# Turning attention probabilities: two 128-lane VectorE transposes and 16 ScalarE copies in place of 16 32-lane VectorE transposes

## The chip, the core and the metric

The kernel runs on one core of one Trainium2 chip. The metric is the device time of one execution in microseconds (us); the value shown is the median of the timed runs. All operands in memory are fp32.

## The reference

Attention with keys and values averaged over groups of 8 positions, and then a feed-forward block with softplus, for batch 8, 8 heads, 576 positions, head size 64 (4608 tokens of 512 numbers, inner size 2048):

```python
k_p = k.reshape(B, H, 72, 8, D).mean(axis=3)
v_p = v.reshape(B, H, 72, 8, D).mean(axis=3)
scores = (q @ k_p.transpose(0, 1, 3, 2)) / sqrt(D)
attn = exp(scores - scores.max(-1))
attn = attn / (attn.sum(-1) + 1e-09)
x = (attn @ v_p) laid out as [B * S, H * D]
h = x @ w_in
g = maximum(h, 0) + log1p(exp(-abs(h)))
out = g @ w_out
```

## The kernel before, in words

The 4608 tokens are cut into 18 chunks of 256 (two tiles of 128 tokens, T = 2). For each chunk there is an attention part and a feed-forward part. The feed-forward part splits every fp32 operand into a high and a low part and multiplies three times. From chunk 4 on (NF) its second product goes through seven smaller products of sums (`pair2_fast`). A chunk has eight steps u of the feed-forward part; a step is 24 matmuls of the first product (`pair1`, line 771) and 21 of the second (`pair2_fast`, line 911). TensorE (PE) runs the first product of step u + 1 ahead of the second product of step u, so that the engines between the two have one step's time. That work between is, per step: on ScalarE (ACT) the softplus `g` (779), the same rounded, `gh` (793), and the rounded sums `so` (836); on VectorE (DVE) the sums `sf` (829 to 831), `gl` (800) and the low part of `so` (841).

While chunk c is in its feed-forward part, the attention of chunk c + 1 is worked through beside it. Its scores stand in a tile E of 128 tokens by 16 rows of (half of the heads, head pair, tile, parity r) by 72 pooled keys. `exponential` (328) raises them, `sum` (579) and `reciprocal` (583, 584) give one factor for each of the 16 rows, and `scale` (603) multiplies. For the product with the values (`av_products`, 690 for the first 64 pooled keys, 697 for the last 8), P must stand with the keys on the partitions, in the tile pT. From chunk 6 on (WIDE), that is done without TensorE:

- `scale(0, False)` (608) is one VectorE instruction over the 8 rows of parity 0; `scale(n, True)` (606) is one ScalarE instruction for each of the 8 rows of parity 1.
- `turn_main` (638) is 16 VectorE transposes. Each takes one quarter of the partitions (32 tokens, i) and 32 of the 64 keys of one parity (f), for all 8 blocks, and writes them to partitions 32f to 32f + 31 of pT, so it crosses from quarter i to quarter f.
- `ends_of` (614), `turn_ends` (622), `ends_high` (627), `ends_low` (631) and `last_high` (663) do the same for the last 8 keys. They are as before after the change.

On TensorE the attention of the next chunk stands between steps 6 and 7 of a chunk: first the scores of chunk c + 1 (518; two small pieces of them are copied out of PSUM by line 552 on VectorE and line 550 on ScalarE), then `av_products(c + 1)`, both in one fixed order with the feed-forward steps (`before`). Chunk 17, the last, has only the `av_products` there.

What each engine does in which order is worked out when the kernel is built, by a list planner (`Order.run`, line 53): every operation has an engine, an estimated cost, operations that it follows, and buffers ("slots") out of named kinds. The planner takes the engine on which something could end first, and on it, of what could start within a pause, the operation with the longest chain of costs behind it; `first` adds to that rank (HURRY, 60, for the feed-forward work on ScalarE and VectorE). The transposes have no such addition. Slots of kind G are six tiles of 512 fp32 per partition, used by `g`, `sf`, the output tiles, `kept` and `le`. On the chip each engine then runs its list in that order, and waits on semaphores for the other engines.

Of the kernel before, what the change touches and what calls it, by code (L numbers as in the profile page):

```python
# [9 lines left out]
F32 = mybir.dt.float32  # L10
# [3 lines left out]
ALU = mybir.AluOpType  # L14
# [16 lines left out]
class Order:  # L31
# [11 lines left out]
    def op(self, engine, cost, fn, after=(), slots=(), lag=None, rest=0, first=0, table=None):  # L43
        o = Op(engine, cost, fn, after, slots, self.HOP if lag is None else lag, len(self.ops))
        o.rest, o.first, o.table = rest, first + self.first, table
        for x in o.after:
            x.followers.append(o)
        for x in slots:
            x.users.append(o)
        self.ops.append(o)  # L50
        return o
# [54 lines left out]
def pooled_attention_softplus_ffn(  # L106
# [9 lines left out]
    nc = tc.nc  # L116
    nc.scalar.preload_act_table_set("exp_and_others")
    B, H, S, D = q.shape
    NTOK, DM = out.shape
    DFF = w_in.shape[1]  # L120
    P = 128
    POOL = 8
    SP = S // POOL
    KM = 64
    KL = SP - KM
    T = 2
    CT = T * P
    HP = H // 2
# [17 lines left out]
    one = ctx.enter_context(tc.tile_pool(name="one", bufs=1))  # L146
# [167 lines left out]
    qt_, x_, e_, pt_, last_ = {}, {}, {}, {}, {}  # L314
# [3 lines left out]
    def ones():  # L318
        x = one.tile([P, T, H, SP], F32, tag="E", name="ones").rearrange("p t h y -> p (t h y)")
        nc.vector.memset(x[:, 0:512], 1.0)  # L320
        return x
# [5 lines left out]
    def exponential(E):  # L327
        nc.scalar.activation(out=E, in_=E, func=AF.Exp, scale=-1.0)
# [175 lines left out]
    class Chunk:  # L504
# [95 lines left out]
                    in0=split(self.E()[:, :, KM:SP])[:, e],  # L600
                    in1=split(self.sm.unsqueeze(2).to_broadcast([P, T * H, KL]))[:, e], op=ALU.mult)

        def scale(self, n, by_scalar):
            r = slice(n, None, 2)
            if by_scalar:
                nc.scalar.mul(self.E()[:, n], self.E()[:, n], self.sm[:, n:n + 1])
            else:
                nc.vector.tensor_tensor(
                    out=self.E()[:, r], in0=self.E()[:, r],
                    in1=self.sm[:, r].unsqueeze(2).to_broadcast([P, T * HP, SP]), op=ALU.mult)  # L610

        def ends_of(self, tag):
            self.pe = one.tile([P, 2 * T, R], F32, tag=tag, name="pe")
# [17 lines left out]
            nc.vector.tensor_tensor(out=x[R:2 * R], in0=self.le[0:R], in1=x[0:R].bitcast(F32),  # L631
                                    op=ALU.subtract)

        def turn_main(self, i, f):
            if i == f == 0:
                pt_[self.c] = one.tile([P, HP, CT], F32, tag="Z", name="pT")
            r, w = slice(32 * i, 32 * (i + 1)), slice(f % 2 * 32, f % 2 * 32 + 32)
            nc.vector.transpose(  # L638
                out=pt_[self.c].rearrange("p n (t i) -> p (n t) i", t=T)[32 * f:32 * f + 32, :, r],
                in_=self.E().rearrange("p (b r) y -> p b r y", r=2)[r, :, f // 2, w])  # L640

        def PT(self, pss):
            for t, ps in enumerate(pss):
# [290 lines left out]
    def load_wi(c, u):  # L934

        for k in range(2):
# [10 lines left out]
    op = todo.op  # L947
    ACT, DVE, PE, SYNC, POOLQ = (nc.scalar.engine, nc.vector.engine, nc.tensor.engine, nc.sync.engine,
                                 nc.gpsimd.engine)
# [9 lines left out]
    def act(n):  # L959
        return 0.14 + 0.00094 * n  # L960
# [4 lines left out]
    def dve2(n):  # L965
        return 0.14 + 0.00106 * n
# [384 lines left out]
    o = op(DVE, 0.3, lambda: x_w.append(ones()), first=2000)  # L1351
# [117 lines left out]
    op = todo.op  # L1469
# [102 lines left out]
    def probabilities(c, where):  # L1572
        x, s_E, subs = chunks[c]
        ex = op(ACT, 1.2 + TABLE, lambda: exponential(e_[c]), [*subs, where], [s_E])
        op(ACT, TABLE, lambda: None, [ex], first=5000)
        s_lt, s_pT, s_sm, s_pe = Slot("lt_"), Slot("pT"), Slot("sm"), Slot("ld")
        s_pm = [Slot("G") for _ in range(0 if c >= WIDE else T)]
        o = op(DVE, 1.33, lambda: x.sum(s_sm.name), [ex], [s_E, s_sm])
        o = op(DVE, 0.4, x.reciprocal, [o], [s_sm])
        if c >= WIDE:  # L1580
            s_le = Slot("G")
            parts = [op(DVE, dve2(576), lambda: x.scale(0, False), [o], [s_E, s_sm])]
            parts += [op(ACT, 0.25, lambda n=n: x.scale(n, True), [o], [s_E, s_sm])
                      for n in range(1, T * H, 2)]
            e = op(ACT, 0.25, lambda: x.ends_of(s_pe.name), parts, [s_E, s_pe])
            main = [op(DVE, dve2(256), lambda i=i, f=f: x.turn_main(i, f),
                       parts[:1] if f < 2 else parts[1:], [s_E, s_pT])
                    for i in range(P // 32) for f in range(4)]
            le = [op(DVE, 0.3, lambda i=i: x.turn_ends(i, s_le.name), [e], [s_pe, s_le])
                  for i in range(P // 32)]  # L1590
            h = op(ACT, act(512), x.ends_high, le, [s_le, s_lt])
            lo = op(DVE, dve2(512), x.ends_low, [h], [s_le, s_lt])
            again = op(ACT, act(512), lambda: x.last_high(2, None), [h], [s_lt])
            late_values[c] = [*main, lo, again], s_lt, s_pT
            return
        e = [op(DVE, 0.7, lambda t=t: x.main(t, s_pm[t].name), [o], [s_E, s_sm, s_pm[t]])
             for t in range(T)]
        e.append(op(DVE, 0.3, lambda: x.ends(s_pe.name), [o], [s_E, s_sm, s_pe]))
        chosen[c] = x, e, s_pm, s_pe, s_lt, s_pT
# [168 lines left out]
    for c in range(N1, NCH + 1):  # L1768
# [5 lines left out]
        for u in range(FP):  # L1774
# [6 lines left out]
            if c < NCH:  # L1781
                if u == 1 and c + 1 <= ALONE + 1:
                    only_scores(c + 1, before if c > N1 else None)
                before = first_products(c, u, before)
                if u == (SOON if c + 1 >= max(WIDE, ALONE + 2) else EXP) and c + 1 < NCH:
                    probabilities(c + 1, third[c, u])
                    if c + 1 <= ALONE:
                        turn_p(c + 1)
                        values(c + 1)
                if u == 4 and ALONE <= c < NCH - 1:  # L1790
                    before = turn_p(c + 1, before)
# [44 lines left out]
```

## Time and profile before

| | us |
|---|---|
| three timed runs | 867.51, 872.35, 879.10 |
| median | 872.35 |
| span of the profiled execution, first to last instruction | 867.6 |
| TensorE busy in it | 846.9 (98%) |
| VectorE busy | 738.7 (85%) |
| ScalarE busy | 422.4 (49%) |
| twelve stretches in which chunks 6 to 17 get their attention (284.77 to 819.57) | 534.8 |

The profiled execution has no time of its own beside its span; the span lies 0.1 us from the lowest timed run and 4.7 us under the median. Busy time of TensorE is not work at its peak: matmuls are pipelined and their ends are modelled, so a short wait can hide inside a busy stretch and shows better as a later start of the next group.

### The profile page before, as it was taken

The numbers are of one execution on the slowest core, as the hardware profiler recorded it, in microseconds if no ns is written. First come the engines' busy times: TensorE is split into PE (matmuls) and PEld (weight loads), VectorE is DVE, ScalarE is ACT, GpSimd is POOL, SyncE is SP. The second block draws the span as 40 slices with busy tenths as digits, with TensorE's granted clock in tenths as the row PEclk, the third lists the DMA queues.
The fourth block names the chain that finished last, engine by engine and source line by source line (L and its number), as shares of the span: only waits on it lengthen the run. The fifth ranks groups of instructions, "written<-read, shape, count | busy, mean of one in ns | idle before, by whom it ended". The sixth has DMA issues, their size and how long they took to land.

```text
span 867.6 us, 20471 instructions
## 1 busy us (share of the span) xinstructions
PE 846.9 (98%) x8056; PEld 803.5 (93%) x8056; DVE 738.7 (85%) x1609; ACT 422.4 (49%) x912; POOL 157.0 (18%) x291
## 2 busy tenths in 40 slices
PE   7999999999999999999999999999999999999997
PEld 3789989889889999999999999999999999999997
DVE  5999999878896898988899999999998997878654
ACT  5954433354444635363735455445545463636332
POOL 1000000004632313021522234123512130000000
PEclk9999999999999999999999999999999999999999
DMA  8974634546788768685677767595769574647572
GB/s 241 318 243 159 206 122 140 186 173 187 245 287 268 238 227 262 227 262 207 220 262 241 257 202 272 198 278 186 272 201 279 191 241 173 232 159 243 184 248 76
DMA packets 88704, 191.14 MB, mean 220 GB/s; under 512 B 23328, under 2 KB 39712, under 8 KB 88608
## 3 DMA queue, kind: packets, MB, share of 16 engines
q1 hardware_dynamic: 79904, 183.00, 63.3%
q0 software_dynamic: 8704, 6.83, 3.1%
q8 instruction: 63, 1.03, 0.5%
q14 instruction: 33, 0.27, 0.1%
HBM read 167.25 MB, written 22.54 MB: 219 GB/s over the span
## 4 chain that ended last, share of the span: by engine, by line
PE 88%; DVE 5%; DMA 3%; ACT 2%; issue 1%; SPq 0%; DVEq 0%; ACTq 0%
PE h L771 36%; PE m L911 29%; PE acc L745 7%; PE h L723 7%; PE avp L690 2%; PE acc L812 2%; DMA w<-wi 2%; PE avp L697 1%; ACT E L440 1%; DMA t<-t 1%; PE sc L518 1%; DMA q<-in_q_dram 1%; PE kps L1150 1%; DVE pT L638 1%; DVE kst L227 0%
## 5 line engine op out<-in xcount | busy, mean ns | idle before, releaser
L771 PE MATMUL h<-x,w 128*128 128x256 f32 x2880 | 349.0, 277 | 1.5 <-DVE x L707 1.2
L771 PEld LDWEIGHTS h<-x,w 128*128 128x128 f32 x2880 | 337.8, 188 | 3.1 <-issue 1.6
L373 POOL DMA_DIRECT2D q<-in_q_dram x272 | 154.6, 572 | 558.5 <-DMA w<-t 192.2
L911 PE MATMUL m<-w,so 128*128 128x256 f32 x1344 | 174.3, 277 | 0.5 <-ACT so L836 0.2
L779 ACT ACTIVATE g<-h 128x512 f32<-128x512 f32 x120 | 71.9, 600 | 205.3 <-PE h L771 205.0
L911 PEld LDWEIGHTS m<-w,so 128*128 128x128 f32 x1344 | 162.6, 188 | 1.2 <-ACT so L836 0.4
L911 PE MATMUL m<-w,gh 128*128 128x256 f32 x672 | 126.2, 277 | 0.0
L836 ACT CAST so<-sf 128x512 fp32r<-128x512 f32 x112 | 69.5, 621 | 80.8 <-DVE sf L831 73.3
L911 PEld LDWEIGHTS m<-w,gh 128*128 128x128 f32 x672 | 101.5, 188 | 0.0
L841 DVE TENSOR_TENSOR so<-sf,so 128x512 fp32r<-128x512 f32 x112 | 77.1, 689 | 22.2 <-ACT so L836 21.3
L911 PE MATMUL m<-w,gl 128*128 128x256 f32 x336 | 93.0, 277 | 0.0
L638 DVE STREAM_TRANSPOSE pT<-E 32x256 f32<-32x256 f32 x192 | 83.7, 436 | 3.1
L829 DVE TENSOR_TENSOR sf<-g 128x256 f32<-128x256 f32 x112 | 47.5, 424 | 42.0 <-ACT g L779 38.8
L723 PEld LDWEIGHTS h<-x,w 128*128 128x128 f32 x576 | 71.8, 188 | 3.6 <-DVE w L1051 0.6
L723 PE MATMUL h<-x,w 128*128 128x256 f32 x576 | 73.2, 279 | 0.3 <-DVE w L1051 0.3
L800 DVE TENSOR_TENSOR gl<-g,gh 128x384 fp32r<-128x384 f32 (+1 forms) x120 | 67.1, 559 | 1.3 <-ACT w L877 0.8
L728 ACT ACTIVATE g<-h 128x256 fp32r<-128x256 f32 x96 | 32.2, 383 | 65.6 <-PE h L723 46.2
L911 PEld LDWEIGHTS m<-w,gl 128*128 128x128 f32 x336 | 63.2, 188 | 0.0
L745 PE MATMUL acc<-w,g 128*128 128x512 f32 x192 | 60.9, 398 | 0.0
L793 ACT ACTIVATE gh<-h 128x384 fp32r<-128x384 f32 (+1 forms) x120 | 59.1, 493 | 0.0
L932 DVE TENSOR_TENSOR o<-o,m 128x256 f32<-128x256 f32 x98 | 39.6, 417 | 3.3 <-ACT o L924 0.4
L745 PEld LDWEIGHTS acc<-w,g 128*128 128x128 f32 x192 | 33.3, 188 | 5.4
(215 smaller groups left out, 977.9 us busy)
## 6 DMA issues: line engine op xcount, KB each, us to landing
w<-wi SPq DMA_DIRECT2D x224, 512.0 KB
out_dram<-o SPq DMA_DIRECT2D x36, 256.0 KB
wst<-in_moe_w_in_dram SPq DMA_DIRECT2D x32, 256.0 KB
wst<-in_moe_w_out_dram SPq DMA_DIRECT2D x16, 512.0 KB
wi<-w SPq DMA_DIRECT2D x16, 512.0 KB
kst<-in_k_dram SPq DMA_DIRECT2D x24, 288.0 KB
vst<-in_v_dram SPq DMA_DIRECT2D x24, 256.0 KB
t<-t SPq DMA_DIRECT2D x9, 512.0 KB
```

Source lines behind the costliest of these rows:

```text
L373: nc.gpsimd.dma_start(out=q_quarters(c)[32 * f:32 * (f + 1), m, g], in_=src[2 * m + f // 2, :, :, f % 2 * 32:f % 2 * 32 + 32])
L638: nc.vector.transpose(out=pt_[self.c].rearrange("p n (t i) -> p (n t) i", t=T)[32 * f:32 * f + 32, :, r], in_=self.E().rearrange("p (b r) ...
L723: nc.tensor.matmul(out=ps[:, 0:CT], lhsT=row(w, kc), rhs=x[:, kc], start=first and kc == j == 0, stop=last and kc == KC - 1 and j == 2)
L745: nc.tensor.matmul(out=accs[c][t], lhsT=a[:, ts], rhs=w, start=f == 0 and j == 0, stop=f == FC - 1 and j == 2)
L771: nc.tensor.matmul(out=ps[:, k * CT:(k + 1) * CT], lhsT=row(w, kc), rhs=x_[c][i][:, kc], start=first and n == 0, stop=last and n == len(or ...
L779: nc.scalar.activation(out=g, in_=x.rearrange("p (b i) -> p b i", i=P), func=AF.Softplus)
L793: nc.scalar.activation(out=gh, in_=quarters(c, x.rearrange("p (b i) -> p b i", i=P)), func=AF.Softplus)
L800: nc.vector.tensor_tensor(out=gl, in0=quarters(c, g), in1=gh.bitcast(F32), op=ALU.subtract)
L829: tt(out=sf[:, 0:3:2], in0=g[:, 0:1].to_broadcast([P, 2, P]), in1=g[:, 1:3], op=ALU.subtract)
L836: nc.scalar.copy(out=so[:, 0], in_=ss[c, u])
L841: nc.vector.tensor_tensor(out=so[:, 1], in0=sf, in1=so[:, 0].bitcast(F32), op=ALU.subtract)
L911: nc.tensor.matmul(out=ms[c][n], lhsT=x, rhs=y, start=u == 0 and j == 0 and n in (1, 6, 5, 4), stop=u == FP - 1 and j == 2 and n in (2, 7, ...
```

## The change

From chunk 6 on, both parities are scaled by one VectorE instruction each. Then for each parity r one VectorE transpose over all 128 partitions (`turn_in`) turns the 32 by 32 blocks in place of quarters into a new tile pq (512 fp32 per partition, a G slot), and eight ScalarE copies (`spread`) carry each 32-partition quarter of pq, 256 numbers a partition, to the quarter of pT where it belongs. The planner is told 0.38 us for each copy.

```diff
-        def scale(self, n, by_scalar):
+        def scale(self, n):
             r = slice(n, None, 2)
-            if by_scalar:
-                nc.scalar.mul(self.E()[:, n], self.E()[:, n], self.sm[:, n:n + 1])
-            else:
-                nc.vector.tensor_tensor(
+            nc.vector.tensor_tensor(
...
-        def turn_main(self, i, f):
-            if i == f == 0:
+        def turn_in(self, r, tag):
+
+            x = self.pm[r] = one.tile([P, T * HP, 2, 32], F32, tag=tag, name="pq")
+            nc.vector.transpose(
+                out=x, in_=self.E().rearrange("p (b r) y -> p b r y", r=2)[:, :, r, 0:KM].rearrange(
+                    "p b (k w) -> p b k w", w=32))
+
+        def spread(self, r, k, i):
+            if self.c not in pt_:
                 pt_[self.c] = one.tile([P, HP, CT], F32, tag="Z", name="pT")
-            r, w = slice(32 * i, 32 * (i + 1)), slice(f % 2 * 32, f % 2 * 32 + 32)
-            nc.vector.transpose(
-                out=pt_[self.c].rearrange("p n (t i) -> p (n t) i", t=T)[32 * f:32 * f + 32, :, r],
-                in_=self.E().rearrange("p (b r) y -> p b r y", r=2)[r, :, f // 2, w])
+            f, w = 2 * r + k, slice(32 * i, 32 * (i + 1))
+            nc.scalar.copy(
+                out=pt_[self.c].rearrange("p n (t i) -> p (n t) i", t=T)[32 * f:32 * f + 32, :, w],
+                in_=self.pm[r][w, :, k])
...
-            parts = [op(DVE, dve2(576), lambda: x.scale(0, False), [o], [s_E, s_sm])]
-            parts += [op(ACT, 0.25, lambda n=n: x.scale(n, True), [o], [s_E, s_sm])
-                      for n in range(1, T * H, 2)]
+            parts = [op(DVE, dve2(576), lambda n=n: x.scale(n), [o], [s_E, s_sm]) for n in range(2)]
             e = op(ACT, 0.25, lambda: x.ends_of(s_pe.name), parts, [s_E, s_pe])
-            main = [op(DVE, dve2(256), lambda i=i, f=f: x.turn_main(i, f),
-                       parts[:1] if f < 2 else parts[1:], [s_E, s_pT])
-                    for i in range(P // 32) for f in range(4)]
+            main = []
+            for r in range(2):
+                s_r = Slot("G")
+                o = op(DVE, dve2(512), lambda r=r, s=s_r: x.turn_in(r, s.name), [parts[r]], [s_E, s_r])
+                main += [op(ACT, 0.38, lambda r=r, k=k, i=i: x.spread(r, k, i), [o], [s_r, s_pT])
+                         for k in range(2) for i in range(P // 32)]
```

## Rows read from the trace of the kernel before

**Rows 1.** The page: its first line and busy time of TensorE.
```profile
span 867.6 us, 20471 instructions
...
PE 846.9 (98%) x8056; PEld 803.5 (93%) x8056; DVE 738.7 (85%) x1609; ACT 422.4 (49%) x912; POOL 157.0 (18%) x291
```

**Rows 2.** Busy time by stretch, one per chunk: stretch, its length, busy us (instructions) of PE, PEld, DVE, ACT, POOL; PEclk.
```profile
461.17:505.23 44.06, 44.06 (x450) 43.26 (x450) 40.60 (x95) 21.80 (x44) 9.30 (x16) 1.00 0.75 243
...
819.57:867.60 48.03, 43.41 (x381) 43.07 (x380) 24.85 (x59) 14.43 (x28) 0.00 (x0) 0.99 0.50 175
sum 582.83, PE 574.19 PEld 565.31 DVE 497.04 ACT 284.83 POOL 116.84; mean PE 44.17 PEld 43.49 DVE 38.23 ACT 21.91 POOL 8.99
```

**Rows 3.** Waits of TensorE from 250 to 850: us in total, times, longest.
```profile
PE avp L690 <- DVE pT L638: 3.6, 5, 0.9
```

**Rows 4.** TensorE timeline: value products of chunks 6, 11, 15; start, us, group.
```profile
321.45 1.06 PE L690 MATMUL avp<-pT,vs 64*64 64x192 f32 x32
322.45 1.08 PE L697 MATMUL avp<-lt__4006,vlo 96*128 96x192 f32 x8
...
541.91 0.60 PE L690 MATMUL avp<-pT,vs 64*64 64x64 f32 x10
...
544.05 1.14 PE L697 MATMUL avp<-lt__7318,vlo 96*128 96x64 f32 x8
...
723.34 0.48 PE L690 MATMUL avp<-pT,vs 64*64 64x192 f32 x2
...
725.69 1.08 PE L697 MATMUL avp<-lt__10006,vlo 96*128 96x192 f32 x8
```

**Rows 5.** Groups of instructions by line: busy us, mean ns, idle before.
```profile
L638 DVE STREAM_TRANSPOSE pT<-E 32x256 f32<-32x256 f32 x192 | 83.7, 436 | 3.1
...
L606 ACT ACTIVATE E<-E,sm 128x72 f32<-128x72 f32 x96 | 25.8, 345 | 0.0
...
L377 DVE STREAM_TRANSPOSE qT<-q 128x512 f32<-128x512 f32 x26 | 18.0, 701 | 5.9 <-DMA q<-in_q_dram 5.8
...
L608 DVE TENSOR_TENSOR E<-E,sm 128x576 f32<-128x576 f32 x12 | 9.0, 754 | 0.2
...
L244 ACT ACTIVATE vs<-vp 128x256 f32<-128x256 f32 x4 | 1.7, 418 | 0.0
...
L663 ACT CAST lt__8668<-lt__8668 32x512 fp32r<-32x512 f32 x1 | 0.6, 617 | 0.0
```

**Rows 6.** ScalarE timeline, chunk 13's attention; in brackets idle before, and what ended it.
```profile
611.08 2.08 ACT L606 ACTIVATE E<-E,sm 128x72 f32<-128x72 f32 x8
...
617.13 0.62 ACT L627 CAST lt__8668<-le 32x512 fp32r<-32x512 f32 x1 [0.59 <-DVE le L622]
...
620.55 0.62 ACT L836 CAST so<-sf 128x512 fp32r<-128x512 f32 x1 [0.99 <-DVE sf L831]
623.68 0.60 ACT L779 ACTIVATE g<-h 128x512 f32<-128x512 f32 x1 [2.51 <-PE h L771]
...
625.75 0.62 ACT L836 CAST so<-sf 128x512 fp32r<-128x512 f32 x1 [1.08 <-DVE sf L831]
628.78 0.60 ACT L779 ACTIVATE g<-h 128x512 f32<-128x512 f32 x1 [2.41 <-PE h L771]
...
631.01 0.62 ACT L836 CAST so<-sf 128x512 fp32r<-128x512 f32 x1 [1.25 <-DVE sf L831]
```

**Rows 7.** VectorE timeline near chunk 13's value products.
```profile
626.40 0.69 DVE L841 TENSOR_TENSOR so<-sf,so 128x512 fp32r<-128x512 f32 x1 [0.22 <-ACT so L836]
...
632.36 0.89 DVE L638 STREAM_TRANSPOSE pT<-E 32x256 f32<-32x256 f32 x2
```

**Rows 8.** TensorE timeline, chunk 13: first use of `so`, start of the value products.
```profile
629.26 1.52 PE L911 MATMUL m<-w,so 128*128 128x256 f32 x12
...
632.10 0.38 PE L690 MATMUL avp<-pT,vs 64*64 64x128 f32 x2
633.40 1.10 PE L690 MATMUL avp<-pT,vs 64*64 64x128 f32 x30 [0.93 <-DVE pT L638]
```

More of the change, by code (lines that the diff above doesn't have):

```diff
@@ L601, in ends @@
                     in1=split(self.sm.unsqueeze(2).to_broadcast([P, T * H, KL]))[:, e], op=ALU.mult)
-        def scale(self, n, by_scalar):
+        def scale(self, n):
             r = slice(n, None, 2)
-            if by_scalar:
-                nc.scalar.mul(self.E()[:, n], self.E()[:, n], self.sm[:, n:n + 1])
-            else:
-                nc.vector.tensor_tensor(
-                    out=self.E()[:, r], in0=self.E()[:, r],
-                    in1=self.sm[:, r].unsqueeze(2).to_broadcast([P, T * HP, SP]), op=ALU.mult)
+            nc.vector.tensor_tensor(
+                out=self.E()[:, r], in0=self.E()[:, r],
+                in1=self.sm[:, r].unsqueeze(2).to_broadcast([P, T * HP, SP]), op=ALU.mult)
         def ends_of(self, tag):
```

## The prediction

> **What bounds the kernel now.** I read the page first: TensorE is busy for 846.9 of 867.6 us [rows 1]. A mean over stages says little, so next I cut the stage that the change touches into stretches of one chunk each. In the stretch of chunk 10 TensorE is busy for all of its 44.06 us, VectorE for 40.60 and ScalarE for 21.80, at a granted clock of 1.00 [rows 2]. So the reader is to see a TensorE that is fed without a break, a VectorE that is nearly full without deciding, and a half idle ScalarE. Taking work off VectorE can pay only where TensorE waits for it.
>
> Third, I asked the waits of TensorE in this stage. One counts: the products with the values wait for the turned P of line 638, 3.6 us in 5 waits [rows 3]. Fourth, since the modelled ends of matmuls hide part of a wait, I measured these places by starts. For chunk 6, which doesn't wait, the 32 products of line 690 take from 321.45 to 322.45, 1.00 us; for chunk 11 they take 2.14 (541.91 to 544.05) and for chunk 15 2.35 (723.34 to 725.69) [rows 4]. That is 1.14 and 1.35 us lost. There are five such places, chunks 11 to 15, all between these two values, so about 5 x 1.25 = 6.2 us. A sixth, chunk 9, loses under 0.3 us by the same measure. So 3.6 us are lost at least, and about 6.5 us at most.
>
> The VectorE timeline at chunk 13 shows why: the last two transposes run from 632.36 to 633.25, behind a `so`, while TensorE is ready at 632.10 and goes on at 633.40 [rows 7, 8]. VectorE simply has not finished by then.
>
> **The change part by part, for each of twelve chunks.**
>
> *VectorE.* Removed: 16 transposes at 436 ns, 6.98 us. Added: two transposes of 128 x 512; line 377 is that size and takes 701 ns, so 1.40 us. Added too: the scaling of the second parity, another 128 x 576 at 754 ns [rows 5]. Net 6.98 - 1.40 - 0.75 = 4.8 us less of VectorE per chunk, 58 us in all. Those 58 us lie beside TensorE's products and are worth nothing by themselves; what counts is the wait of up to 6.5 us that they removed or didn't.
>
> *ScalarE.* Removed: eight multiplications, 2.08 us in a row [rows 6]. Added: 16 copies of 32 x 256. The trace has no such copy. Below it lies the 128 x 72 instruction, which comes every 0.26 us (2.08 / 8) [rows 6]. Beside it lies a 128 x 256 ScalarE instruction, 418 ns; above it lies a 32 x 512 cast, 617 ns, which also shows that 32 lanes are no cheaper than the 600 to 620 ns of a 128 x 512 [rows 5, 6]. I take 0.42, the same number of columns; the ends are 0.26 and 0.62. So 16 x 0.42 = 6.7 us (4.2 to 9.9), net 4.6 us more per chunk, and ScalarE goes from some 22 to some 26.5 us of 44 [rows 2].
>
> *Do the copies fit?* Chunk 13: the multiplications end at 613.16, and the second transpose can be through about 1.5 us later. From there to the value products at 632.10 ScalarE has gaps of 0.59, 0.99, 2.51, 1.08, 2.41 and 1.25 us, 8.8 us together [rows 6]. In whole copies of 0.42 these take 1 + 2 + 5 + 2 + 5 + 2 = 17, and 16 are wanted. It just fits even if no copy pushes anything. A copy may also push: `so` ends at 627.09 on VectorE and is first used by TensorE at 629.26 [rows 7, 8], 2.2 us later, while one copy in front of `g` and one in front of `so` delay it by 0.8 us at most. That cover is TensorE's own 5.1 us step; if it were gone, each pushed copy would cost 0.4 us.
>
> *The new tile.* pq takes two of the six G slots for some microseconds, and the transpose must find one free. It stands in VectorE's queue, and if it waits there, the `sf`, `gl` and `so` behind it wait too, and so does TensorE. Per step of 5.1 us, `g` and `sf` hold about one slot each for half the time, `le` one more, so about three are free. I cost this at nothing; below nothing it can't be, since a taken slot frees no one, and above it is bounded by the 2.2 us of slack before anything shows.
>
> *What is late next.* With P in time the value products start when the scores end. The two small score pieces have to be out of PSUM by then; chunk 6 shows that they are [rows 4].
>
> *Sum.* 867.6 - 6.5 = 861.1 us against the profiled execution. The median of the runs lies 4.7 us above that execution, and no row tells why; I carry it: 861.1 + 4.7 = 865.8, say 866 us.
>
> **A rule weighed.** The row says that TensorE's matmuls are busy for all of chunk 10's 44.06 us, and its weight loads for 43.26; over the twelve stretches up to 819.57 the lengths add up to 582.83 - 48.03 = 534.8 us and the weight loads to 565.31 - 43.07 = 522.2 [rows 2]. The Trainium skill, "Perfetto Trace Analysis", section "Identifying the Most-Contended Engine", says that busy matmuls are no good measure of how near TensorE is to its limit, and that the busy share of weight loads is. By that the room is 534.8 - 522.2 = 12.6 us and not 6.5. The trace agrees only in part: chunk 10, which waits for nothing, still keeps 44.06 - 43.26 = 0.8 us apart, and 12 x 0.8 would be most of it.
>
> **The rivals.**
>
> *A: more comes back than the visible wait.* If all time of the twelve stretches outside weight loads was caused by a slow VectorE, the span falls to 867.6 - 12.6 = 855.0, the median to about 860. For it: the two measures of the wait, 3.6 and 6.5, differ already. Against: the 0.8 us of the chunk that waits for nothing.
>
> *B: nothing comes back.* The wait stays and has a new name, the last copy in place of the last transpose, because the planner places the copies as filler like the transposes. Then the time is that of before, 872, with 869 where half comes back. For it: the transposes were planned to be in time, too, and weren't. Against: ScalarE had 8.8 us of gaps, VectorE next to none.
>
> *C: the other side, the copies are too dear.* If crossing quarters makes a 256 copy cost what a 32 x 512 cast costs, 0.62 us, the gaps of chunk 13 take 0 + 1 + 4 + 1 + 3 + 2 = 11 of 16. Five, 3.1 us, have to push or stand in front of the value products. It decides from 8.8 / 16 = 0.55 us a copy. At 1 to 3 us late in each of 12 chunks that is 12 to 36 us, less the 6.5: between 878 and 902 us, 890 in the middle. Against: the transposes that it replaces cross quarters at 436 ns, and a 32-lane cast from quarter to quarter takes what 128 lanes take.
>
> *D: the change doesn't relieve what waits.* That is the case if the last transposes were late for their place in the order and not for VectorE's load. The 0.89 us at 632.36 stand right behind a `so`; a lightly loaded VectorE with the same last place would be as late. It gives 872 again, and I count it with B.
>
> **How the numbers follow.** Forecast (waits gone, copies hidden): 0.65. A: 0.07. B and D: 0.18. C: 0.10. The forecast by itself spans 863 (all of the 6.5, and 3 us less of what the median carries over its best run) to 870 (half of the 3.6 and nothing else). The range for 8 in 10 reaches into A and B and to the lower edge of C: 859 to 876 us. Two per cent, about what a measurement of this kernel can tell from no change, is 17.4 us: faster than 854.9 not even A reaches; I leave 0.03 for it. Slower than 889.8 is half of C, 0.05, and 0.01 for a stall on the G slots. The rest, 0.91, is within 2%.
>
> **What would show each step.** VectorE's busy time should fall by about 58 us, to 680, and ScalarE's rise by about 55, to 477. Line 638 should vanish, with two 128 x 512 transposes of about 0.70 us and 16 copies of about 0.42 us per chunk in its place. The value products of chunks 11 to 15 should take 1.0 us by starts, and TensorE should have no wait of that line. A wait of the value products for the copies would show B; copies of 0.55 us or more, and `g` or `so` later against TensorE, would show C; shorter stretches in chunks that didn't wait before would show A. The prediction is wrong if the stage from 284.77 to 819.57 doesn't shrink by 4 to 8 us.

## The result and the profile after

The kernel with the change takes 862.92 us (median of 4 runs, 861.82 to 863.30) against 871.05 us (median of 4); the ratio is 0.988, 95% interval 0.985 to 0.992. A second measurement, with 10 runs of the change and 19 of before on another chip, gave 866.64 against 872.57 us, ratio 0.992 (0.989 to 0.995). So the change saves 6 to 8 us, some 1%: inside the 2% band, and clear of noise. The profiled execution took 863.26 us with a span of 861.5; so 1.8 us lie around the span.

The page of the kernel after, first line, busy time, and the row of the new copies (columns as in [rows 5], idle time behind the bar):

```profile
span 861.5 us, 20428 instructions
...
PE 843.8 (98%) x8056; PEld 802.9 (93%) x8056; DVE 678.2 (79%) x1453; ACT 476.2 (55%) x1008; POOL 156.8 (18%) x291
...
L642 ACT COPY pT<-pq 32x256 f32<-32x256 f32 x192 | 77.5, 404 | 5.6 <-DVE pq L634 2.9
```

VectorE's busy time fell by 60.5 us against [rows 1], and ScalarE's rose by 53.8; the span fell by 6.1. So a tenth of what was taken off VectorE came back as time in this execution.

The waits of TensorE from 250 to 850 in the kernel after (us in total, times, longest), against [rows 3]:

```profile
PE m L915 <- ACT so L840: 1.1, 1, 1.1
PE h L775 <- DMA w<-wi: 0.6, 2, 0.4
PE avp L694 <- DVE kept L552: 0.3, 1, 0.3
PE m L915 <- DVE so L845: 0.2, 1, 0.2
```

The wait of the value products for P is gone, and nothing stands in its place: not for a copy, not for a transpose. The timeline of TensorE in the kernel after says the same by starts; these are the value products of chunks 11 and 15, which took 2.14 and 2.35 us before [rows 4]:

```profile
541.65 1.06 PE L694 MATMUL avp<-pT,vs 64*64 64x64 f32 x32
542.65 1.14 PE L701 MATMUL avp<-lt__7277,vlo 96*128 96x64 f32 x8
...
720.15 1.06 PE L694 MATMUL avp<-pT,vs 64*64 64x192 f32 x32
721.15 1.08 PE L701 MATMUL avp<-lt__9949,vlo 96*128 96x192 f32 x8
```

Now they take 1.00 us each, like chunk 6 before. All twelve lie between 0.97 and 1.03; by starts that is 6.6 us less than before over the stage.

The whole stage by the windows view (stretch, its length, busy us of PE, PEld, DVE, ACT, POOL, granted clock), first before:

```profile
284.77:819.57 534.80, 530.78 (x5363) 522.24 (x5362) 472.19 (x1080) 270.40 (x538) 116.84 (x206) 1.00 0.69 229
```

and after:

```profile
285.87:813.44 527.57, 526.98 (x5362) 520.12 (x5362) 411.64 (x924) 324.30 (x634) 116.72 (x206) 1.00 0.70 232
```

The stage is 7.2 us shorter, at the same granted clock. The stage begins 1.1 us later than before; 0.9 us of that is one wait of line 915 for a `so` at 269.85, 1.10 us here and 0.23 before. The end behind the stage is the same, 48.06 against 48.03 us [rows 2].

One execution is a rough measure, though. A second profiled execution of the kernel after had a span of 866.2 us. From the start of chunk 5's value products to that of chunk 17's it took 529.93 us, where the first took 527.65 and the kernel before 534.88; three waits for weights (`w<-wi`), 2.4 us together, are about the difference between the two. All twelve value products lay between 0.97 and 1.02 us there too. So the stage is 5 to 7 us shorter.

Where the copies went, in ScalarE's timeline of the kernel after, chunk 13 (as [rows 6], idle before in brackets):

```profile
620.00 0.62 ACT L840 CAST so<-sf 128x512 fp32r<-128x512 f32 x1
620.64 2.89 ACT L642 COPY pT<-pq 32x256 f32<-32x256 f32 x7
623.56 0.60 ACT L783 ACTIVATE g<-h 128x512 f32<-128x512 f32 x1
624.05 0.49 ACT L797 ACTIVATE gh<-h 128x384 fp32r<-128x384 f32 x1
624.57 0.40 ACT L642 COPY pT<-pq 32x256 f32<-32x256 f32 x1
625.30 0.62 ACT L840 CAST so<-sf 128x512 fp32r<-128x512 f32 x1 [0.33 <-DVE sf L835]
628.33 0.60 ACT L783 ACTIVATE g<-h 128x512 f32<-128x512 f32 x1 [2.41 <-PE h L775]
```

Seven copies fill the gap of 2.51 us that stood ahead of `g` before, and the last copy ends at 624.97, while the value products start at 631.60. So there are 6.6 us to spare, and the gap ahead of the next `g` is empty again. VectorE's new transposes found a free G slot each time; they had 0.1 us of idle time ahead of them in all 24 (behind the last bar):

```profile
L634 DVE STREAM_TRANSPOSE pq<-E 128x512 f32<-128x512 f32 x24 | 16.7, 702 | 0.1
```

### The profile page after: what moved, and what is told of

Same layout as the page of the kernel before. It is cut to its first block, busy times and chain, and to the rows that moved or that the text cites. A ratio compares the mean times of both kernels' runs of the same rounds, so it can differ in the third digit from the quotient of the medians.

```text
span 861.5 us, 20428 instructions
## 1 busy us (share of the span) xinstructions
PE 843.8 (98%) x8056; PEld 802.9 (93%) x8056; DVE 678.2 (79%) x1453; ACT 476.2 (55%) x1008; POOL 156.8 (18%) x291
## 3 DMA queue, kind: packets, MB, share of 16 engines
q8 instruction: 63, 1.03, 0.5%
## 4 chain that ended last, share of the span: by engine, by line
PE 85%; DMA 6%; DVE 4%; issue 2%; POOL 1%; ACT 1%; SPq 1%; ACTq 0%; POOLq 0%; DVEq 0%
PE h L775 34%; PE m L915 29%; PE h L727 8%; PE acc L749 8%; DMA w<-wi 3%; PE avp L694 2%; PE avp L701 1%; POOL q L373 1%; PE sc L518 1%; DMA q<-in_q_dram 1%; DMA t<-t 1%; DMA kvst<-in_v_dram 1%; PE vps L1171 1%; ACT E L440 1%; DVE d L869 1%
## 5 line engine op out<-in xcount | busy, mean ns | idle before, releaser
L642 ACT COPY pT<-pq 32x256 f32<-32x256 f32 x192 | 77.5, 404 | 5.6 <-DVE pq L634 2.9
```

The source lines that it names most:

```text
L642: nc.scalar.copy(out=pt_[self.c].rearrange("p n (t i) -> p (n t) i", t=T)[32 * f:32 * f + 32, :, w], in_=self.pm[r][w, :, k])
```

## The experiments

Three theories were held apart. Theory 1, that of the prediction: only P's lateness at the value products costs, and VectorE was late because of what it had to do. Theory 2: the transposes were late only by their place in VectorE's order. Theory 3: any relief of VectorE shortens the stage.

**One part alone: both parities scaled by VectorE, the 16 transposes kept.**

```diff
-            parts += [op(ACT, 0.25, lambda n=n: x.scale(n, True), [o], [s_E, s_sm])
-                      for n in range(1, T * H, 2)]
+            parts += [op(DVE, dve2(576), lambda: x.scale(1, False), [o], [s_E, s_sm])]
```

> The kernel before with one part of the change alone: both parities are scaled by VectorE (8 ScalarE multiplications of 2.1 us become one VectorE instruction of 0.75 us per chunk), the 16 transposes stay. Theory 1, the value products wait because VectorE has too much to do before them: the wait for the transposes grows from 3.6 us in 5 waits to 6 to 10 us in 7 to 12 waits, and the time by 2 to 9 us (ratio to before 1.002 to 1.010). Theory 2, the transposes are late only because of their place in VectorE's order: no change within 2 us. Theory 3, any relief of VectorE shortens the stage by itself, about 8 us for 58 us: 12 x 0.75 us more costs 1.2 us, and the wait for the transposes stays at 3.6 us.

884.70 against 874.24 us, ratio 1.011 (1.005 to 1.018). The first line of TensorE's waits in this run:

```profile
PE avp L690 <- DVE pT L638: 8.0, 12, 1.0
```

The wait went from 3.6 us in 5 to 8.0 in 12, now in seven chunks: 0.75 us more on VectorE ahead of each chunk's transposes makes more chunks late, and later. Theory 1 stands for the wait; the time, 10.5 us more, is a little above its 2 to 9. Theories 2 and 3 are off. The 4.4 us of added waits are under half of the loss. A part of the rest is the clock behind two of these waits. These are the first products behind the value products of chunks 12 and 13:

```profile
605.41 2.88 PE L771 MATMUL h<-x,w 128*128 128x256 f32 x24
...
653.65 3.98 PE L771 MATMUL h<-x,w 128*128 128x256 f32 x24
```

The granted clock was 1.00 from 604 to 612, but 0.50 from 650 to 654; the 15 matmuls of line 911 ahead of it and the 24 of this product took 7.1 us by starts in chunk 13 and 4.4 in chunk 12. Behind chunk 11's waits it was 0.50, too, from 554 to 556. So the one part of the change that loads VectorE is a loss by itself, and the two must go together.

**No work changed, the transposes put forward.**

```diff
-            if i == f == 0:
+            if self.c not in pt_:
...
-                       parts[:1] if f < 2 else parts[1:], [s_E, s_pT])
+                       parts[:1] if f < 2 else parts[1:], [s_E, s_pT], first=HURRY)
```

The first pair only lets whichever transpose comes first make the tile pT.

> The kernel before with no work changed: the 16 transposes get the planner's addition HURRY, so that they stand earlier in VectorE's order. Theory 1 (VectorE's load): the wait for the transposes is gone, but what they displace comes late in its turn, so half of the gain at most: ratio to before 0.994 to 1.003. Theory 2 (the place in the order): the same gain as the change, ratio 0.985 to 0.992, with no new wait. Theory 3 (relief as such): ratio 1.000, since no work is taken from VectorE.

871.22 against 874.24 us, ratio 0.998 (0.994 to 1.001). Waits of TensorE, from 250 to 880, the first three:

```profile
PE m L911 <- ACT so L836: 1.5, 1, 1.5
PE h L771 <- DVE x L707: 1.0, 2, 0.8
PE m L911 <- DVE gl L800: 0.9, 1, 0.9
```

Not one wait for line 638 is left, so the place in the order alone is enough to remove it; this much of theory 2 is right. The gain is not there: the interval of the ratio takes in 1. The wait for `so`, at 268.74, stands ahead of the stage, where other executions have one, too (0.2 us before, 1.1 and 2.0 in the two of the kernel after). In the stage, small waits for x and `gl` came, 1.9 us together, and 38 of 111 steps ran at a slower pace (last section), 19 more than in the kernel before, which at 0.2 us each is 3.8 us. The wait for `gl` follows a late transfer of q, for which VectorE stood:

```profile
641.53 0.71 DVE L377 STREAM_TRANSPOSE qT<-q 128x512 f32<-128x512 f32 x1 [2.60 <-DMA q<-in_q_dram]
```

So the trace doesn't show that the transposes displaced other work, as theory 1 expected; the new order put a transpose of q in front of step work. Why the pace was slower is open, and with it most of why this kernel gained nothing.

**Half of the change.** Parity 0 goes the new way, parity 1 keeps eight 32-lane transposes (`turn_main` is put back, not shown):

```diff
-            main = []
-            for r in range(2):
+            main = [op(DVE, dve2(256), lambda i=i, f=f: x.turn_main(i, f), parts[1:], [s_E, s_pT])
+                    for i in range(P // 32) for f in (2, 3)]
+            for r in range(1):
```

> The change for parity 0 alone; parity 1 keeps its eight 32-lane transposes, scaled by VectorE. VectorE loses 8 x 0.436 - 0.70 - 0.75 = 2.0 us per chunk in place of 4.8. Theory 1: the waits were 1.14 to 1.35 us, less than 2.0, so they are gone altogether, and the ratio is that of the change, 0.986 to 0.992. Theory 2: the last transposes still stand where they stood, so the wait stays, 2 to 4 us, ratio 0.995 to 1.000. Theory 3: the gain goes by the work taken away, 2.0 of 4.8, so 3.4 us, ratio 0.996.

864.72 against 874.24 us, ratio 0.989 (0.982 to 0.996). All waits of TensorE from 250 to 880:

```profile
PE m L923 <- ACT so L848: 2.9, 1, 2.9
PE h L783 <- DMA w<-wi: 1.1, 3, 0.5
```

Two microseconds less on VectorE per chunk do as much as 4.8. The ratio alone hardly tells this from the 0.996 of theory 3; that no value product waits, with less than half of the relief, does. So the gain doesn't go by the work that is taken away; it is had as soon as the last transpose is in time, and no more was had.

**VectorE loaded again, three ways.** Four sums per chunk that nobody reads were added to the kernel after (the helpers that make them are not shown). First over E, after the exponential:

```diff
+            for n in range(4):
+                s_n = Slot("mn")
+                op(DVE, 1.33, lambda s=s_n: x.sum_again(s.name), [ex], [s_E, s_n])
```

> The kernel after with VectorE loaded again as it was: four more sums over E per chunk (4 x 1.35 = 5.4 us), whose results nobody reads and which nothing follows. The output stays the reference's. Theory 1: P is turned early all the same, so the time is that of the change within 2 us, ratio to before 0.986 to 0.992, with no wait of the value products. Theory 3 (relief as such): the gain is given back, ratio 0.998 to 1.002.

898.36 against 874.24 us, ratio 1.027 (1.021 to 1.033), with 15.8 us of waits of the value products for copies. That is far beyond what theory 3 expected, so it can't have been the load alone. The sums were then made to follow all that VectorE does for P (against the first loaded kernel):

```diff
-                op(DVE, 1.33, lambda s=s_n: x.sum_again(s.name), [ex], [s_E, s_n])
+                op(DVE, 1.33, lambda s=s_n: x.sum_again(s.name), [o, lo], [s_E, s_n])
```

> The same four sums per chunk (5.4 us of VectorE) as in the loaded kernel, whose results nobody reads, but planned to follow all that VectorE does for P (the second 128-lane transpose and the low part of the last 8 keys), so that they don't stand ahead of it. Theory 1 (only P's lateness costs): no wait of the value products, time within 3 us of the kernel after, ratio to before 0.986 to 0.994. Theory 3 (relief as such): the gain is given back, ratio 0.998 or more.

897.20 against 872.57 us, ratio 1.030 (1.026 to 1.035), the same. VectorE's timeline in this run shows why, up to the value products of chunk 10:

```profile
479.43 1.34 DVE L583 TENSOR_REDUCE again<-E 128x16 f32<-128x1152 f32 x1
480.81 1.27 DVE L570 TENSOR_TENSOR E<-sc,mn 128x504 f32<-128x504 f32 x2
...
495.81 1.30 DVE L638 STREAM_TRANSPOSE pq<-E 128x512 f32<-128x512 f32 x2
```

and ScalarE's:

```profile
499.67 6.61 ACT L646 COPY pT<-pq 32x256 f32<-32x256 f32 x16
```

E is one buffer. The last unread sum over the old E ends at 480.77, and only then can line 570 write the next chunk's scores into E; in the kernel after it did so for the same chunk from 455.54 on. Everything for P is late from there, and all 16 copies stand in one row at the very end, 499.67 to 506.28, while the scores on TensorE were through at about 500. In the first loaded kernel the last unread sum stands at 481.94, and line 570 at 483.31. So both runs delayed P by way of E, which I hadn't thought of; they show what a late P costs, and say nothing on load. So the third way sums over a constant tile:

```diff
+            for n in range(4):
+                s_n = Slot("mn")
+                op(DVE, 1.2, lambda s=s_n: x.idle_sum(s.name), [ex], [s_n])
```

> The kernel after with VectorE loaded again, by work that holds nothing: four sums over a constant tile per chunk (128 x 1024 each, about 1.2 us, 4.8 us together), read by nobody. The two loaded kernels so far summed over E, and so kept the next chunk's scores out of E and made P late by another way. Theory 1 (only lateness of P or of a step's own work costs; VectorE's load by itself nothing): no wait of the value products, within 3 us of the kernel after, ratio to before 0.986 to 0.996. Theory 3 (relief as such): the gain is given back, ratio 0.998 to 1.002 or more.

865.33 against 874.51 us, ratio 0.991 (0.987 to 0.994). The page's busy line:

```profile
PE 845.7 (98%) x8056; PEld 805.0 (93%) x8056; DVE 731.1 (85%) x1501; ACT 475.8 (55%) x1008; POOL 156.7 (18%) x291
```

and all waits of TensorE from 250 to 950:

```profile
PE m L920 <- ACT so L845: 2.0, 1, 2.0
PE h L780 <- DMA w<-wi: 0.3, 1, 0.3
PE avp L699 <- DVE kept L552: 0.3, 1, 0.3
PE m L920 <- DVE so L850: 0.2, 1, 0.2
```

VectorE is nearly as busy as before the change, 731.1 against 738.7 us, and the gain is kept. Theory 3 is out: VectorE's load cost nothing here, where it stood behind P's transposes (for chunk 10 these ran at 485.22, and the next three sums from 492.40 to 498.35).

This run and the half also rule out that the gain is one of pace. Of their steps in the stage 20 and 19 ran at the slower pace of the last section, as many as the 18 of the kernel before. Yet from chunk 5's value products to chunk 17's they took 529.53 and 529.58 us, 5.3 less than before.

**The copies twice as dear.** Each copy is made twice:

```diff
-            nc.scalar.copy(
+            for _ in range(2):
+                nc.scalar.copy(
...
```

> The kernel after with each ScalarE copy made twice and the planner not told, so that a copy costs 0.8 us in place of 0.41. The output stays the reference's. By rival C as the prediction priced it, the copies decide from 0.55 us on: the value products wait 1 to 3 us for the copies in every chunk, ratio to before 1.005 to 1.03. By the trace of the kernel after, the last copy of chunk 13 ends at 624.97 and the products start at 631.60, so 16 x 0.41 = 6.6 us more just fit: waits of under 1 us in few chunks, ratio 0.986 to 0.996.

923.92 against 872.57 us, ratio 1.062 (1.056 to 1.068): dearer than both readings. The waits of TensorE, the first two and the fourth:

```profile
PE m L916 <- ACT gh L798: 13.2, 9, 1.8
PE m L916 <- DVE gl L805: 7.7, 11, 0.7
...
PE m L916 <- ACT so L841: 2.6, 4, 1.4
```

ScalarE's timeline in one such chunk:

```profile
511.48 4.23 ACT L643 COPY pT<-pq 32x256 f32<-32x256 f32 x10
515.74 0.60 ACT L784 ACTIVATE g<-h 128x512 f32<-128x512 f32 x1
```

The value products don't wait for a copy at all. The planner, told 0.38 us, packed five copies into a gap for five; at twice the price they run on for 4.23 us and push the softplus behind them, and with it the next step on TensorE. A row of copies ahead of `g` is one block, not one copy of 0.4 us. All waits of TensorE from 250 on are 32 of the 51 us; behind waits at seven places of the stage the granted clock fell to 0.50 (from 420 to 422, for one), which is a part of the rest. To tell the planner's ignorance from a full ScalarE, it was told the price:

```diff
-                main += [op(ACT, 0.38, lambda r=r, k=k, i=i: x.spread(r, k, i), [o], [s_r, s_pT])
+                main += [op(ACT, 0.8, lambda r=r, k=k, i=i: x.spread(r, k, i), [o], [s_r, s_pT])
```

> The kernel with each copy made twice, but the planner told 0.8 us in place of 0.38. If the 50 us that the double copies cost came from ScalarE being full (rival C's reading), the time stays over 1.04 of before. If they came from copies that the planner, told 0.38, packed in front of the softplus of the next step, the packing is undone and ScalarE's 33 of 44 us per chunk still fit: few waits for gh and gl, ratio 0.99 to 1.015.

906.41 against 874.51 us, ratio 1.037 (1.032 to 1.043): short of the full ScalarE's 1.04, but far nearer to it than to the 0.99 to 1.015. The first line of TensorE's waits:

```profile
PE avp L695 <- ACT pT L643: 17.6, 11, 3.9
```

The waits for `gh` and `gl` are gone, so the packing had caused them; in their place the value products wait for the copies in 11 of 12 chunks, by starts mostly 2.0 us each and 25 us together. That is rival C of the prediction in its place, and at its price for the wait (12 to 36 us); the time lies above its 878 to 902, and a part of that is again the granted clock, at 0.50 from 328 to 338 behind the longest of these waits, 3.9 us.

**The same for chunk 5.** `WIDE = 5` in place of 6.

> The kernel after with the same way of turning P for chunk 5 too (WIDE = 5 in place of 6), which takes that chunk's ten transposes off TensorE (10 x 0.11 us) and its copies out of PSUM. Theory 1: 1 us less than the kernel after, if nothing in chunk 4's step becomes late; too small to be told by the times, so the stretch of chunk 4's steps is what to read. Rival: chunk 4 has more beside it (its VectorE is fuller), so the value products of chunk 5 wait for the copies, 0 to 2 us more.

873.43 against 872.57 us, ratio 1.000 (0.996 to 1.003): the gain is lost. TensorE's longest wait, and VectorE's row behind it:

```profile
PE m L915 <- DVE gl L804: 12.6, 1, 12.6
```

```profile
264.54 0.71 DVE L377 STREAM_TRANSPOSE qT<-q 128x512 f32<-128x512 f32 x1 [14.15 <-DMA q<-in_q_dram]
```

The planner put a transpose of q ahead of step work in VectorE's order, and the transfer of q landed late; VectorE stood for 14 us, and TensorE with it. This execution took 876.61 us, 3.2 more than the median, so the wait need not be as long in each. No theory foresaw it: the loss seen is not at the value products (1.0 us each from chunk 6 on), but at a wait that a new order put in front of other work. No version tried here beats the kernel after.

## Why the prediction was right, and where it was off

- *What bounds.* Right: the wait of line 638 was what could be won on VectorE. The 58 us that were said to be "worth nothing by themselves" measured 60.5, and with 53 us of them put back as the free load the gain stayed (ratio 0.991). One run is left over: with only the order changed the wait went, too, and the time hardly moved.
- *The size.* 6.5 us were forecast; the waits by starts gave 6.6, the stage 7.2 in one execution and 5.0 in the other, the span 6.1 and 1.4, the two comparisons of medians 8.1 and 5.9. The measure by starts was right and the 3.6 us of the waits view too low. The stage's other 0.6 us in the first lies within what the slow steps of the last section make (18 in the stage before, 11 after, at 0.2 us). That the sum's 861.1 us met a span of 861.5 is in part luck: the second execution's span was 866.2.
- *The term that was mis-sized* is the 4.7 us "that the median carries": 1.8 of them lie around the span (1.7 to 2.1 in every execution for which time and span are on record), so that the 0.1 us between the span before and its lowest timed run says nothing. The rest, what a run has above the profiled execution, was 0 in the first measurement (863.26 profiled, 862.92 median) and 3.4 in the second (863.26 against 866.64). So 866 came out as 862.9 and 866.6; what a run has above the profiled one is open.
- *ScalarE.* A copy was taken at 0.42 and measured 0.404, a 128 x 512 transpose at 0.701 and measured 0.702; 55 us were said to be added, 53.8 were. That the copies just fit the gaps was too cautious: in chunk 13 they were done 6.6 us ahead of the value products.
- *The new tile.* "I cost this at nothing" held: 0.1 us of idle time of VectorE ahead of all 24 transposes.
- *Rival C.* The mechanism is real and the price of its wait was right (2.0 us in most chunks where 1 to 3 were said), but the point from which it decides was probably too low: with copies of 0.83 us, planned as such, 2.0 us were missing, so by an estimate 13.3 - 2.0 = 11.3 us fit, or 0.7 us a copy in place of 0.55. No run had copies of that price. And the step "a copy pushes by 0.8 us at most" holds only while the planner's cost is right; packed blind, the copies pushed by their whole row.
- *Rival D* was "counted with B" at 872. Its mechanism was half right: put forward, the transposes are in time without any work taken away; but that kernel's time came out at 0.998 of before. D's forecast that the change would leave the wait was wrong, since it was gone.
- *Rival A and the rule.* The room outside weight loads shrank from 12.6 to 527.57 - 520.12 = 7.5 us, though no wait of note is left. So by this trace the rule of the Trainium skill ("Perfetto Trace Analysis", "Identifying the Most-Contended Engine") marks a room of which 0.6 us per chunk isn't waits; chunk 10's 0.8 had shown that.

## What to carry to other kernels

Measure a wait in front of a pipelined engine by the starts of the groups around it, and take that as about what relief of the other engine can return; the engine's whole relief, ten times as much here, is no measure. Work moved onto a half idle engine was free here only while it stayed clear of that engine's short deadlines: the price that the planner is told decides whether it lands in a gap or in front of the next step. And a filler that only reads a buffer still holds it, and can delay whoever writes it next.

## What had not been expected of the hardware

**Two paces at one granted clock.** TensorE's timeline of the kernel after, one step of 24 matmuls in each pace:

```profile
548.94 2.99 PE L775 MATMUL h<-x,w 128*128 128x256 f32 x24
...
591.35 2.88 PE L775 MATMUL h<-x,w 128*128 128x256 f32 x24
```

By starts of steps it is 5.30 against 5.10 us for a step of 45 matmuls, so 4% for whole stretches, with the granted clock at 1.00 in both (in the second execution over the slow 549 to 590 and the fast 595 to 630, and in the kernel before over the slow 732 to 769). That second execution of the kernel after had the slow pace again behind the value products of chunks 11 and 13, and once more, behind a transfer, in chunk 9's steps; so did the half and the freely loaded kernel behind chunks 11 and 13, but not the kernel before, where those products waited. So some of it seems to go with the program. It mostly changes at the scores and value products or at a wait, but not always: at 660.21 in the kernel after it changed inside an unbroken row of steps. What sets it is open. It makes some 2 to 8 us between executions and kernels here.

**A wait can cost twice.** The windows view of the kernel with the late sums, from the wait in chunk 10 on:

```profile
490.00:500.00 10.00, 10.00 (x137) 9.87 (x140) 9.28 (x21) 5.21 (x12) 0.00 (x0) 1.00 0.61 218
500.00:503.00 3.00, 0.33 (x23) 0.18 (x12) 2.91 (x6) 2.90 (x9) 0.18 (x1) 0.89 0.75 234
503.00:509.00 6.00, 3.78 (x19) 1.83 (x20) 3.95 (x8) 3.20 (x8) 5.93 (x12) 0.50 0.13 28
509.00:513.00 4.00, 4.00 (x23) 4.00 (x22) 3.27 (x4) 1.07 (x2) 3.77 (x8) 0.55 0.14 31
513.00:520.00 7.00, 7.00 (x64) 7.00 (x63) 4.18 (x10) 2.68 (x6) 6.57 (x12) 1.00 0.61 184
```

TensorE's idle stretches of 2.69 and 2.21 us, from about 500 on, took the granted clock from 1.00 (2.4 GHz) to 0.50 (1.2 GHz) for about 10 us. From these value products to the next the chunk took 50.9 us, 7.4 more than the 43.5 of the same chunk in the kernel after, of which the wait itself was 5.22 - 0.97 = 4.25. The five waits of the kernel before, 1.1 to 1.4 us each, left the clock at 1.00 over the stage, and so cost their length and no more. But the length of the wait doesn't tell which it will be. With both parities scaled by VectorE, chunk 13's two idle stretches of 1.04 and 0.52 us took the clock to 0.50, and chunk 15's of 1.04 and 0.42 us left it at 1.00; in the kernel with the copies planned at 0.8 us, chunk 13's 1.55 us took it down, and chunk 17's 2.37 us didn't.

**Copies in a row don't overlap.** Sixteen copies took 6.61 us, 0.413 each, a little over their own 404 ns; the eight multiplications took 2.08 us, 0.26 each, less than their own 345 ns [rows 5, 6]. The prediction's upper bound of 0.62, from a 32-lane cast of twice the columns, was not near.
